# Attention decode step with gated Mish block: 4 MB loads in five buffers, wider projections and one merge of the row maxima

## Chip, cores and metric

The kernel runs on one core of a Trainium2 chip. The metric is the device time of one execution in microseconds. Before the change the median of three timed runs is 225.47 us (225.37 to 225.68). All data are float32.

## What is computed

Two batch rows, one new token each. `A` is attention over the last W = 4096 positions of a cache with 8 key/value heads, each shared by 4 of the 32 query heads; `B` is a two-layer block with a Mish activation; a scalar gate per batch row mixes them.

```
W = 4096; rep = 4; Dh = 128; D = 512; F = 1792
q = (x @ wq).reshape(B, 1, 32, 128).transpose(0, 2, 1, 3)
k = repeat(k_cache[:, :, Sk - W:, :], rep, axis=1)
v = repeat(v_cache[:, :, Sk - W:, :], rep, axis=1)
p = softmax(einsum("bhqd,bhkd->bhqk", q, k) * Dh ** -0.5)
a = einsum("bhqk,bhkd->bhqd", p, v).transpose(0, 2, 1, 3).reshape(B, 1, 4096) @ wo
h = x @ w1 + b1
b = (h * tanh(softplus(h))) @ w2
g = sigmoid((x * gate_w).sum(-1, keepdims=True))
out = g * a + (1 - g) * b
```

The host cuts and reorders the arrays before the launch, so that each load reads one contiguous piece of memory, with one contiguous row per partition.

## The kernel before, in words

**Loads.** Every large input goes through `load` (L49), which takes one of 20 buffers of 128 x 2048 floats (1 MB, a row of 8 KB per partition) and issues one DMA on SyncE (SP) at L51. For each of the 8 key/value heads there are four loads of keys (`k`, transposed on the host), four of values (`v`), one of the query weights (`wq`) and one of the output weights (`wo`). The hidden weights `w1` come in four loads of 896 KB, `w2` in nine loads cut at `CUTS` (L35), the last five of 256 KB with rows of 2 KB. SP issues in program order; a tile framework adds the waits for free buffers. With `sm`, a load of 13 KB that holds x, the gate weights and the bias, and the store of the result, there are 95 DMAs.

**Compute.** `x32` is x, padded to 32 columns, so that a matmul writes a group of 32 output partitions; four groups `j` make 128 partitions. `queries` (L113) projects x for one head: 16 matmuls of 128 columns, a copy, a transpose and two copies into `qz`. `softmax` (L130) makes the scores in 16 matmuls of 512 columns (L134), takes each row's maximum (L138), merges the maxima of the partitions that hold parts of the same row by a matmul and a masked minimum (L140, L143), and takes the exponential with its sum (L147); L149 to L154 make the reciprocal of the sum times the gate. `values` (L157) transposes the probabilities (L161), copies them (L162), does 16 matmuls of 512 columns with the values (L166), copies the result (L170) and gathers the diagonal blocks by four small matmuls (L177). `project` (L184) multiplies by `wo`: for each of the four query heads four matmuls of 128 columns into `acc`, through `accumulate` (L94). `hidden` (L188) does the first layer and Mish; `output` (L239) adds the second layer into the same `acc`.

**Order.** The loop at L245 issues, for head kv, its value loads, then the query weights and keys of the next head and that head's softmax, then `values` and `project`. The last head ends with `w2`, interleaved with two `wo` loads; the five 256 KB pieces of `w2` come last. Then four copies on VectorE bring `acc` into `res` (L270), and SP stores it (L271).

Of the kernel before, what the change touches and what calls it, by code (L numbers as in the profile page):

```python
# [8 lines left out]
F32 = mybir.dt.float32  # L9
# [17 lines left out]
Q = 32  # L27
F = 1792
DC = D // P
FC = F // P  # L30
FG = 4
SMALL = DC * B + DC + FC
SCALE = DH ** -0.5
BIG = 3.0e38
CUTS = (0, 2, 5, 7, 9, 10, 11, 12, 13, 14)  # L35
# [3 lines left out]
def decode_kernel(ctx: ExitStack, tc: tile.TileContext, small, wq, kt, v, wo, w1, w2, out):  # L39
# [3 lines left out]
    stream = ctx.enter_context(tc.tile_pool(name="stream", bufs=20))  # L43
# [10 lines left out]
    wq_t = load(wq[0], 2048, "wq0")  # L54
# [4 lines left out]
    b1 = sm[:, DC * B + DC :]  # L59

    ident = const.tile([P, P], F32, name="ident")
    make_identity(nc, ident)
    nident = const.tile([P, P], F32, name="nident")
    nc.vector.tensor_scalar_mul(nident, ident, -SCALE)
    fold = const.tile([P, Q], F32, name="fold")
    nc.vector.tensor_reduce(fold, ident.rearrange("p (j r) -> p r j", r=Q), axis=AX.X, op=ALU.add)
    key = const.tile([P, 2 * B, REP], F32, name="key")
    nc.vector.tensor_tensor(
        key,
        fold.rearrange("p (y n h) -> p y n h", n=NH, h=REP)[:, :, 0, :],  # L70
        fold.rearrange("p (y n h) -> p y n h", n=NH, h=REP)[:, :, 1, :], op=ALU.add)
    mask = const.tile([P, P], F32, name="mask")
    mv = mask.rearrange("p (j y n h) -> p j y n h", j=NJ, n=NH, h=REP)
    for j in range(NJ):
        for n in range(NH):
            nc.vector.tensor_scalar(mv[:, j, :, n, :], key, -BIG, BIG, op0=ALU.mult, op1=ALU.add)
# [11 lines left out]
    nc.gpsimd.memset(actT, 0.0)  # L88

    acc = ps_1.tile([P, P], F32, tag="acc", name="acc")  # L90
    n_acc = HQ + FC
    done = [0]

    def accumulate(lhsT, rhs):  # L94
        for j in range(NJ):
            nc.tensor.matmul(  # L96
                acc[Q * j : Q * j + Q, :], lhsT, rhs[:, j * P : (j + 1) * P],
                start=(done[0] == 0), stop=(done[0] == n_acc - 1),
            )
        done[0] += 1  # L100

    zp = ps_1.tile([P, B], F32, tag="q", name="zp")
    for c in range(DC):
        nc.tensor.matmul(zp, gw[:, c : c + 1].to_broadcast([P, P]), xT[:, c, :],
                         start=(c == 0), stop=(c == DC - 1))
    g = const.tile([P, B], F32, name="g")
    omg = const.tile([P, B], F32, name="omg")
    nc.scalar.activation(g, zp, AF.Exp, scale=-1.0)  # L108
    nc.vector.tensor_scalar_add(g, g, 1.0)
    nc.vector.reciprocal(g, g)  # L110
    nc.vector.tensor_scalar(omg, g, -1.0, 1.0, op0=ALU.mult, op1=ALU.add)

    def queries(kv, wq_t):  # L113
        qp = ps_1.tile([P, DH], F32, tag="q", name=f"qp{kv}")
        w = wq_t.rearrange("p (c n) -> p c n", c=DC)
        for c in range(DC):
            for h in range(REP):
                nc.tensor.matmul(qp[Q * h : Q * h + Q, :], x32[:, c, :],  # L118
                                 w[:, c, h * DH : (h + 1) * DH],
                                 start=(c == 0), stop=(c == DC - 1))  # L120
        qs = work.tile([P, DH], F32, tag="qs", name=f"qs{kv}")
        nc.vector.tensor_copy(qs, qp)
        qt = ps_1.tile([P, REP, Q], F32, tag="q", name=f"qt{kv}")
        nc.tensor.transpose(qt.rearrange("p h r -> p (h r)"), qs, ident)
        for n in range(NH):
            nc.vector.tensor_copy(
                qz[:, kv, :].rearrange("p (b n x) -> p b n x", n=NH, x=Q + REP)[:, :, n, :REP],
                qt.rearrange("p h r -> p r h")[:, :B, :])

    def softmax(kv, kts):  # L130
        sc = ps_s.tile([P, 512], F32, tag="sc", name=f"sc{kv}")
        for m in range(BN):
            for j in range(NJ):
                nc.tensor.matmul(sc[Q * j : Q * j + Q, :], qz[:, kv, m * Q : m * Q + Q],  # L134
                                 kts[m][:, j * 512 : (j + 1) * 512],
                                 start=(m == 0), stop=(m == BN - 1))
        mx = tiny.tile([P, 1], F32, tag="mx", name=f"mx{kv}")
        nc.vector.tensor_reduce(mx, sc, axis=AX.X, op=ALU.max)  # L138
        mb = ps_1.tile([P, P], F32, tag="mb", name=f"mb{kv}")
        nc.tensor.matmul(mb, mx.to_broadcast([P, P]), nident, start=True, stop=True)  # L140
        junk = work.tile([P, P], F32, tag="junk", name=f"junk{kv}")
        bias = tiny.tile([P, 1], F32, tag="bias", name=f"bias{kv}")
        nc.vector.tensor_tensor_reduce(out=junk, in0=mb, in1=mask, op0=ALU.add, op1=ALU.min,  # L143
                                       scale=1.0, scalar=BIG, accum_out=bias)
        p = work.tile([P, 512], F32, tag="p", name=f"p{kv}")
        l = tiny.tile([P, 1], F32, tag="l", name=f"l{kv}")
        nc.scalar.activation(p, sc, AF.Exp, bias=bias, scale=SCALE, accum_out=l)  # L147
        rl = tiny.tile([P, B, REP], F32, tag="rl", name=f"rl{kv}")
        nc.vector.tensor_scalar_mul(rl, key[:, :B, :], l)  # L149
        lp = ps_1.tile([P, B, REP], F32, tag="mb", name=f"lp{kv}")  # L150
        nc.tensor.matmul(lp, ones, rl, start=True, stop=True)  # L151
        r = tiny.tile([P, B, REP], F32, tag="r", name=f"r{kv}")
        nc.vector.reciprocal(r, lp)
        nc.vector.tensor_tensor(r, r, g[:, :, None].to_broadcast([P, B, REP]), op=ALU.mult)  # L154
        return p, r

    def values(kv, p, r, vts, between=None):  # L157
        pp = ps_1.tile([P, NT, P], F32, tag="pt", name=f"pp{kv}")
        pT = work.tile([P, NT, P], F32, tag="pT", name=f"pT{kv}")
        for t in range(NT):  # L160
            nc.tensor.transpose(pp[:, t, :], p[:, t * P : (t + 1) * P], ident)  # L161
        nc.vector.tensor_copy(pT, pp)  # L162
        o = ps_1.tile([P, BN * DH], F32, tag="o", name=f"o{kv}")
        for t in range(NT):
            for j in range(NJ):
                nc.tensor.matmul(o[Q * j : Q * j + Q, :], pT[:, t, Q * j : Q * j + Q],  # L166
                                 vts[t][:, j * 512 : (j + 1) * 512],
                                 start=(t == 0), stop=(t == NT - 1))
        os = work.tile([P, BN * DH], F32, tag="os", name=f"os{kv}")
        nc.scalar.copy(os, o)  # L170
        if between is not None:
            between()
        ol = ps_1.tile([P, B, REP], F32, tag="ol", name=f"ol{kv}")
        for b in range(B):
            for n in range(NH):
                m = b * NH + n
                nc.tensor.matmul(ol[:, b], os[:, m * DH : (m + 1) * DH],  # L177
                                 fold[:, m * REP : (m + 1) * REP],
                                 start=(n == 0), stop=(n == NH - 1))
        nc.vector.tensor_tensor(  # L180
            oT[:, kv * REP : (kv + 1) * REP, :B].rearrange("p h b -> p b h"), ol, r,
            op=ALU.mult)

    def project(kv, wo_t):  # L184
        for h in range(REP):
            accumulate(oT[:, kv * REP + h, :], wo_t[:, h * D : (h + 1) * D])

    def hidden(w1s):  # L188
        hp = ps_1.tile([P, FG * P], F32, tag="pt", name="hp")
        for c in range(DC):  # L190
            for j in range(NJ):
                n = min(FG, FC - j * FG) * P
                nc.tensor.matmul(hp[Q * j : Q * j + Q, :n], x32[:, c, :],  # L193
                                 w1s[c][:, j * FG * P : j * FG * P + n],
                                 start=(c == 0), stop=(c == DC - 1))
        hs = const.tile([P, FG * P], F32, name="hs")
# [3 lines left out]
        ht = ps_1.tile([P, FG, NJ, Q], F32, tag="q", name="ht")  # L200
# [29 lines left out]
    def head(kv, wq_t):  # L230
        kts = [load(kt[kv, m], 2048, f"k{kv}_{m}") for m in range(BN)]
        queries(kv, wq_t)
        return softmax(kv, kts)

    def load_w2(f0, n):
        src = w2[f0 * P * D : (f0 + n) * P * D].rearrange("(p x) -> p x", p=P)
        return f0, n, load(src, n * D, f"w2_{f0}")

    def output(loaded):  # L239
        f0, n, t = loaded  # L240
        for k in range(n):
            accumulate(actT[:, f0 + k, :], t[:, k * D : (k + 1) * D])

    st = head(0, wq_t)
    for kv in range(HKV):  # L245
        vts = [load(v[kv, t], 2048, f"v{kv}_{t}") for t in range(NT)]
        if kv == 1:
            hidden([load(w1[c * P : (c + 1) * P, :], F, f"w1_{c}") for c in range(DC)])
        nxt = head(kv + 1, load(wq[kv + 1], 2048, f"wq{kv + 1}")) if kv + 1 < HKV else None
        if kv < HKV - 2:  # L250
            wo_t = load(wo[kv], REP * D, f"wo{kv}")
        elif kv == HKV - 1:
# [7 lines left out]
        if kv == HKV - 1:  # L260
            project(kv - 1, wo_p)
        if kv != HKV - 2:
            project(kv, wo_t)
# [48 lines left out]
```

## Time and profile before

| what | value |
|---|---|
| median of the timed runs | 225.47 us |
| profiled execution: time shown by its profile (its span) | 223.8 us |
| instructions in the profile | 3067, of them 1316 matmuls and 1316 weight loads |
| PE busy / VectorE / ScalarE | 151.0 / 30.3 / 12.6 us |
| read from memory | 91.24 MB |
| mean granted TensorE clock | 0.794 |

The profiled execution has no timed value of its own; its span is 1.7 us below the median of the timed runs. In the page, the row GB/s gives what the DMA engines moved in 40 equal slices of the span; the row of a queue gives packets, megabytes and the share of the time of 16 DMA engines (where packets overlap a little, that share can pass 100%). A group's row gives busy time, mean duration in ns, and the idle time of the engine before it with what ended it. A row of the waits gives the total in us, how often, and the longest.

### The profile page before, as it was taken

To read this page: it belongs to the slowest core of one execution; us is meant where nothing else is said; L and a number is where in the kernel's file an instruction comes from. 1 tells how busy PE (TensorE), PEld (TensorE's weight loads), DVE (VectorE), ACT (ScalarE), POOL (GpSimd) and SP (SyncE) were. 2 spreads that over 40 slices of the span, in tenths; PEclk is the share of its full clock that TensorE was granted. 3 is DMA by queue.
4 is the path that set the end of the run, shared out by engine and by line. 5 is a ranking of instruction groups with operands and counts; after the bars stand their busy time and mean duration, and the time that the engine had idled before them with its cause. 6 is when DMAs were issued, how large, how long until landed. Compare 5 with 4: busy or idle time off the path is not lost.

```text
span 223.8 us, 3067 instructions
## 1 busy us (share of the span) xinstructions
PE 151.0 (67%) x1316; PEld 59.8 (27%) x1316; DVE 30.3 (14%) x128; ACT 12.6 (6%) x27; POOL 3.0 (1%) x9
## 2 busy tenths in 40 slices
PE   0794477503899687577975787568865786549662
PEld 0622051200043413014240523024322414031440
DVE  0403010200070211012010210021011201030002
ACT  2001010100001101001010101010100000010100
POOL 5000000000000000000000000000000000000000
PEclk9999967965699859855598559955899569955999
DMA  6999999999999999999999999999999999999980
GB/s 235 428 428 428 422 431 426 425 425 423 432 422 425 428 431 425 428 425 429 422 426 426 431 423 426 425 431 425 428 425 429 423 429 425 428 426 425 420 334 7
DMA packets 13552, 91.43 MB, mean 409 GB/s; under 512 B 1634, under 2 KB 1634, under 8 KB 3300
## 3 DMA queue, kind: packets, MB, share of 16 engines
q1 hardware_dynamic: 13540, 91.25, 97.1%
q8 instruction: 10, 0.16, 0.3%
q14 instruction: 2, 0.02, 0.0%
HBM read 91.24 MB, written 0.00 MB: 408 GB/s over the span
## 4 chain that ended last, share of the span: by engine, by line
DMA 96%; PE 1%; SPq 1%; DVE 1%; issue 0%; DVEq 0%
DMA k<-in_kt 49%; DMA v<-in_v 17%; DMA w<-in_w 12%; DMA wo<-in_wo 9%; DMA wq<-in_wq 9%; SPq L51 1%; PE sc L134 0%; DVE res L270 0%; DVE mx L138 0%; PE mb L140 0%; PE acc L96 0%; SPq L56 0%; DVEq L308 0%
## 5 line engine op out<-in xcount | busy, mean ns | idle before, releaser
L134 PE MATMUL sc<-k,qz 128*32 128x512 f32 x256 | 40.5, 717 | 18.7 <-DMA k<-in_kt 16.7
L166 PE MATMUL o<-v,pT 128*32 128x512 f32 x256 | 44.9, 836 | 8.4 <-DVE pT L162 5.5
L166 PEld LDWEIGHTS o<-v,pT 128*32 128x32 f32 x256 | 9.4, 145 | 38.2 <-issue 20.4
L134 PEld LDWEIGHTS sc<-k,qz 128*32 128x32 f32 x256 | 6.9, 120 | 43.1 <-DMA k<-in_kt 28.2
L96 PE MATMUL acc<-wo,oT 128*32 128x128 f32 x256 | 15.7, 355 | 2.2 <-DMA wo<-in_wo 2.2
L193 PE MATMUL hp<-w,x 128*32 128x512 f32 (+1 forms) x32 | 6.8, 853 | 10.1 <-DMA w<-in_w 10.1
L138 DVE TENSOR_REDUCE mx<-sc 128x1 f32<-128x512 f32 x8 | 5.5, 692 | 54.5 <-PE sc L134 54.5
L177 PE MATMUL ol<-fold,os 128*128 128x4 f32 x64 | 8.9, 262 | 4.6 <-ACT os L170 4.5
L177 PEld LDWEIGHTS ol<-fold,os 128*128 128x128 f32 x64 | 8.2, 201 | 11.2 <-ACT os L170 11.2
L96 PEld LDWEIGHTS acc<-wo,oT 128*32 128x32 f32 x256 | 9.8, 135 | 4.4 <-issue 2.7
L147 ACT ACTIVATE p<-sc,bias 128x512 f32<-128x512 f32 x8 | 5.5, 688 | 93.9 <-DVE bias L143 93.9
L118 PE MATMUL qp<-wq,x 128*32 128x128 f32 x256 | 10.4, 312 | 0.3 <-ACT g L108 0.3
L161 PE MATMUL pp<-ident,p 128*128 128x128 f32 x32 | 8.4, 398 | 2.5 <-ACT p L147 2.5
L180 DVE TENSOR_TENSOR oT<-ol,r 128x8 f32<-128x8 f32 x8 | 1.4, 172 | 61.7 <-PE ol L177 61.7
L140 PE MATMUL mb<-nident,mx 128*128 128x128 f32 x16 | 5.2, 417 | 6.5 <-DVE mx L138 6.5
L170 ACT COPY os<-o 128x512 f32<-128x512 f32 x8 | 4.7, 586 | 74.2 <-PE o L166 74.2
L118 PEld LDWEIGHTS qp<-wq,x 128*32 128x32 f32 x256 | 7.7, 124 | 0.9 <-ACT g L108 0.3
L140 PEld LDWEIGHTS mb<-nident,mx 128*128 128x128 f32 x16 | 3.2, 249 | 16.3 <-DVE mx L138 16.3
L162 DVE COPY pT<-pp 128x512 f32<-128x512 f32 x8 | 5.5, 692 | 10.5 <-PE pp L161 10.4
L96 PE MATMUL acc<-w,actT 128*32 128x128 f32 x112 | 4.9, 280 | 2.7 <-DMA w<-in_w 2.6
L161 PEld LDWEIGHTS pp<-ident,p 128*128 128x128 f32 x32 | 5.3, 205 | 4.9 <-ACT p L147 3.0
L151 PE MATMUL lp<-rl,ones 128*128 128x8 f32 x16 | 4.0, 322 | 3.7 <-DVE rl L149 3.7
(56 smaller groups left out, 41.6 us busy)
## 6 DMA issues: line engine op xcount, KB each, us to landing
k<-in_kt SPq DMA_DIRECT2D x32, 1024.0 KB, 19.6
v<-in_v SPq DMA_DIRECT2D x32, 1024.0 KB, 19.6
wq<-in_wq SPq DMA_DIRECT2D x8, 1024.0 KB, 19.6
wo<-in_wo SPq DMA_DIRECT2D x8, 1024.0 KB, 19.6
w<-in_w SPq DMA_DIRECT2D x4, 896.0 KB, 18.9
w<-in_w SPq DMA_DIRECT2D x3, 512.0 KB, 18.0
w<-in_w SPq DMA_DIRECT2D x5, 256.0 KB, 11.0
w<-in_w SPq DMA_DIRECT2D x1, 768.0 KB
```

Of the source, the lines that this page charges most:

```text
L96: nc.tensor.matmul(acc[Q * j : Q * j + Q, :], lhsT, rhs[:, j * P : (j + 1) * P], start=(done[0] == 0), stop=(done[0] == n_acc - 1),)
L118: nc.tensor.matmul(qp[Q * h : Q * h + Q, :], x32[:, c, :], w[:, c, h * DH : (h + 1) * DH], start=(c == 0), stop=(c == DC - 1))
L134: nc.tensor.matmul(sc[Q * j : Q * j + Q, :], qz[:, kv, m * Q : m * Q + Q], kts[m][:, j * 512 : (j + 1) * 512], start=(m == 0), stop=(m == ...
L138: nc.vector.tensor_reduce(mx, sc, axis=AX.X, op=ALU.max)
L140: nc.tensor.matmul(mb, mx.to_broadcast([P, P]), nident, start=True, stop=True)
L147: nc.scalar.activation(p, sc, AF.Exp, bias=bias, scale=SCALE, accum_out=l)
L161: nc.tensor.transpose(pp[:, t, :], p[:, t * P : (t + 1) * P], ident)
L162: nc.vector.tensor_copy(pT, pp)
L166: nc.tensor.matmul(o[Q * j : Q * j + Q, :], pT[:, t, Q * j : Q * j + Q], vts[t][:, j * 512 : (j + 1) * 512], start=(t == 0), stop=(t == NT ...
L170: nc.scalar.copy(os, o)
L177: nc.tensor.matmul(ol[:, b], os[:, m * DH : (m + 1) * DH], fold[:, m * REP : (m + 1) * REP], start=(n == 0), stop=(n == NH - 1))
L193: nc.tensor.matmul(hp[Q * j : Q * j + Q, :n], x32[:, c, :], w1s[c][:, j * FG * P : j * FG * P + n], start=(c == 0), stop=(c == DC - 1))
```

## The change

All tiles of the stream become 128 x 8192 floats (4 MB, a row of 32 KB per partition), in five buffers instead of 20 of a quarter the size. Keys and values are one load per head each, the query weights two loads of four heads each, `w1` one load; `w2` is cut at 10, 12 and 13, and its last three pieces go to buffers of their own. `wo` comes at the end of the stream, in loads of 4, 2, 1 and 1 heads. The host arrays follow these shapes. There are 29 DMAs instead of 95.

`queries` is done twice, for four heads at a time, with 512-column matmuls. `softmax` subtracts each partition's own maximum; the maxima of all heads are merged once at the end, in the new function `weights`, which also makes the factors that correct for it. `values` gathers the diagonal blocks on VectorE (`pick`) instead of PE. `outputs` applies the factors, and `project` does one 512-column matmul per query head into one of four partition groups, which `finish(fold, asum)` adds up at the end. The result's four copies are shared by VectorE and ScalarE. The program has 1,610 PE instructions instead of 2,670.

```diff
-CUTS = (0, 2, 5, 7, 9, 10, 11, 12, 13, 14)
+HALF = 4
+CHUNK = 8192
+CUTS = (0, 10, 12, 13, 14)
...
-    stream = ctx.enter_context(tc.tile_pool(name="stream", bufs=20))
+    stream = ctx.enter_context(tc.tile_pool(name="stream", bufs=5))
...
-        t = stream.tile([P, 2048], F32, tag="s", name=name)
+        t = stream.tile([P, CHUNK], F32, tag="s", name=name)
...
+    def queries(i, t):
+        w = t.rearrange("p (c k n) -> p c k n", c=DC, k=HALF)
+        qp = ps_1.tile([P, REP * DH], F32, tag="o", name=f"qp{i}")
         for c in range(DC):
...
+            for k in range(HALF):
+                nc.tensor.matmul(qp[Q * k : Q * k + Q, :], x32[:, c, :], w[:, c, k, :],
                                  start=(c == 0), stop=(c == DC - 1))
...
+        nc.vector.tensor_reduce(mx[:, kv : kv + 1], sc, axis=AX.X, op=ALU.max)
         bias = tiny.tile([P, 1], F32, tag="bias", name=f"bias{kv}")
...
+        nc.vector.tensor_scalar_mul(bias, mx[:, kv : kv + 1], -SCALE)
         p = work.tile([P, 512], F32, tag="p", name=f"p{kv}")
...
+        nc.scalar.activation(p, sc, AF.Exp, bias=bias, scale=SCALE, accum_out=ls[:, kv : kv + 1])
...
+        d = od[:, kv, :]
+        nc.vector.tensor_scalar_mul(d, o[:, 0, :], pick[:, 0:1])
+        for m in range(1, BN):
+            nc.vector.scalar_tensor_tensor(d, o[:, m, :], pick[:, m : m + 1], d,
+                                           op0=ALU.mult, op1=ALU.add)
...
+    def weights():
+        mt = ps_1.tile([HKV, NJ, Q], F32, tag="q", name="mt")
+        nc.tensor.transpose(mt.rearrange("k j r -> k (j r)"), mx, ident)
...
+        for j in range(NJ):
+            nc.vector.tensor_tensor(mj[:, j], m4[:, j, :, 0, :], m4[:, j, :, 1, :], op=ALU.max)
+        top = const.tile([HKV, Q // NH // REP, REP], F32, name="top")
+        nc.vector.tensor_reduce(top, mj.rearrange("k j y h -> k y h j"), axis=AX.X, op=ALU.max)
+        for j in range(NJ):
+            for n in range(NH):
+                nc.vector.tensor_tensor(m4[:, j, :, n, :], m4[:, j, :, n, :], top, op=ALU.subtract)
+        nc.scalar.activation(ms, ms, AF.Exp, scale=SCALE)
...
+    queries(0, wq_a)
+    queries(1, wq_b)
+    hidden(w1_t)
+
+    for kv in range(HKV - 1):
+        pT = softmax(kv, load(kt[kv], CHUNK, f"k{kv}"))
+        values(kv, pT, load(v[kv], CHUNK, f"v{kv}"))
...
+    w2_0 = load_w2(0)
+    wos = [(k0, k1, load_wo(k0, k1)) for k0, k1 in ((0, 4), (4, 6), (6, 7), (7, 8))]
+    tail = [load_w2(i) for i in range(1, len(CUTS) - 1)]
...
+    def project(j, lhsT, rhs, n):
+        nc.tensor.matmul(acc[Q * j : Q * j + Q, :], lhsT, rhs,
+                         start=(n_col[j] == 0), stop=(n_col[j] == n - 1))
...
+    nc.scalar.copy(asum[:, : D // 2], acc[:, : D // 2])
+    nc.vector.tensor_copy(asum[:, D // 2 :], acc[:, D // 2 :])
...
+    output(1)
+    finish(fold, asum)
+    output(2)
+    output(3)
...
     for j in range(NJ):
-        nc.vector.tensor_copy(res[:, j * P : (j + 1) * P], acc[Q * j : Q * j + B, :])
+        copy = nc.scalar.copy if j % 2 else nc.vector.tensor_copy
+        copy(res[:, j * P : (j + 1) * P], fin[Q * j : Q * j + B, :])
```

On SP, the loads at the start of the program; the number after the partitions is the floats of a row. Before, the query weights of one head, the small load `sm`, and the keys and values of the first head:

```order
L51 DMA wq_73<-in_wq 128x2048
L56 DMA sm<-in_small 128x26
L51 DMA k_0_120<-in_kt 128x2048
L51 DMA k_1_122<-in_kt 128x2048
L51 DMA k_2_124<-in_kt 128x2048
L51 DMA k_3_126<-in_kt 128x2048
L51 DMA v_0_185<-in_v 128x2048
```

After, on SP at the same place:

```order
L53 DMA wqa<-in_wq 128x8192
L58 DMA sm<-in_small 128x26
L53 DMA wqb<-in_wq 128x8192
L53 DMA w_79<-in_w 128x7168
L53 DMA k_231<-in_kt 128x8192
L53 DMA v_262<-in_v 128x8192
L53 DMA k_285<-in_kt 128x8192
```

All query weights and `w1` (`w_79`) now stand ahead of the first keys, and the sixth large load (`k_285`) is the first that reuses a buffer.

On SP, the loads at the end of the program. Before, `w` with an underscore is a piece of `w2`, named by its first block:

```order
L51 DMA wo_1111<-in_wo 128x2048
L51 DMA w_2_1113<-in_w 128x1536
L51 DMA w_5_1115<-in_w 128x1024
L51 DMA w_7_1117<-in_w 128x1024
L51 DMA w_9_1119<-in_w 128x512
L51 DMA w_10_1121<-in_w 128x512
L51 DMA w_11_1123<-in_w 128x512
L51 DMA w_12_1125<-in_w 128x512
L51 DMA w_13_1127<-in_w 128x512
L271 DMA out<-res 2x512
```

After, on SP from the last head's keys on:

```order
L53 DMA k_609<-in_kt 128x8192
L53 DMA v_611<-in_v 128x8192
L53 DMA w_0_613<-in_w 128x5120
L53 DMA wo_615<-in_wo 128x8192
L53 DMA wo_617<-in_wo 128x4096
L53 DMA wo_619<-in_wo 128x2048
L53 DMA wo_621<-in_wo 128x2048
L261 DMA w_10_623<-in_w 128x1024
L261 DMA w_12_625<-in_w 128x512
L261 DMA w_13_627<-in_w 128x512
L322 DMA out<-res 2x512
```

All of `wo` has moved behind the last values, and the last 1 MB is three pieces of `w2` instead of five with 1.25 MB. Counting five buffers back, `wo_619` takes the buffer of the last keys and `wo_621` that of the last values.

On PE, the end of the program after the change, from the last head's scores on (`mt`, `ft`, `lp` belong to `weights`, `ol` to `outputs`):

```order
L130 MATMUL sc_631<-k_609,qz 32x512 x16
L141 MATMUL pp_653<-ident,p_651 128x128 x4
L185 MATMUL lp<-kl,ones 128x64
L195 MATMUL ol<-kf,od 128x8 x7
L149 MATMUL o_706<-v_611,pT_654 32x512 x16
L277 MATMUL acc<-w_0_613,actT 32x512 x10
L277 MATMUL acc<-wo_615,oT 32x512 x16
L277 MATMUL acc<-wo_621,oT 32x512 x4
L287 MATMUL fin<-w_10_623,actT 32x128 x8
L287 MATMUL fin<-asum,fold 32x128 x4
L287 MATMUL fin<-w_12_625,actT 32x128 x4
L287 MATMUL fin<-w_13_627,actT 32x128 x4
```

Where `wo` of a head was used right after that head's values before, all of it is now used here; between the last of it and the last two pieces of `w2` stand the copies into `asum` and the four matmuls that add it up.

More of the change, by code (lines that the diff above doesn't have):

```diff
@@ L88, in decode_kernel @@
     nc.gpsimd.memset(actT, 0.0)
[L90 to L115, printed above, removed]
+    mx = const.tile([P, HKV], F32, name="mx")
+    ls = const.tile([P, HKV], F32, name="ls")
@@ L120, in queries @@
                                  start=(c == 0), stop=(c == DC - 1))
-        qs = work.tile([P, DH], F32, tag="qs", name=f"qs{kv}")
+        qs = work.tile([P, REP * DH], F32, tag="p", name=f"qs{i}")
         nc.vector.tensor_copy(qs, qp)
[L123 to L128, printed above, removed]
@@ L130, in softmax @@
-    def softmax(kv, kts):
+        qt = ps_1.tile([P, REP, HALF, Q], F32, tag="pt", name=f"qt{i}")
+        for h in range(REP):
+            nc.tensor.transpose(qt[:, h].rearrange("p k r -> p (k r)"),
+                                qs[:, h * DH : (h + 1) * DH], ident)
+        for k in range(HALF):
+            for n in range(NH):
+                nc.vector.tensor_copy(
+                    qz[:, i * HALF + k, :].rearrange("p (b n x) -> p b n x", n=NH, x=Q + REP)[:, :, n, :REP],
+                    qt[:, :, k, :B].rearrange("p h b -> p b h"))
@@ L131, in softmax @@
+    def softmax(kv, t):
         sc = ps_s.tile([P, 512], F32, tag="sc", name=f"sc{kv}")
@@ L145, in softmax @@
         p = work.tile([P, 512], F32, tag="p", name=f"p{kv}")
[L146 to L157, printed above, removed]
+        nc.scalar.activation(p, sc, AF.Exp, bias=bias, scale=SCALE, accum_out=ls[:, kv : kv + 1])
         pp = ps_1.tile([P, NT, P], F32, tag="pt", name=f"pp{kv}")
         pT = work.tile([P, NT, P], F32, tag="pT", name=f"pT{kv}")
-        for t in range(NT):
-            nc.tensor.transpose(pp[:, t, :], p[:, t * P : (t + 1) * P], ident)
+        for c in range(NT):
+            nc.tensor.transpose(pp[:, c, :], p[:, c * P : (c + 1) * P], ident)
@@ L162, in values @@
         nc.vector.tensor_copy(pT, pp)
-        o = ps_1.tile([P, BN * DH], F32, tag="o", name=f"o{kv}")
-        for t in range(NT):
+        return pT
+    def values(kv, pT, t):
+        o = ps_1.tile([P, BN, DH], F32, tag="o", name=f"o{kv}")
+        for c in range(NT):
             for j in range(NJ):
-                nc.tensor.matmul(o[Q * j : Q * j + Q, :], pT[:, t, Q * j : Q * j + Q],
-                                 vts[t][:, j * 512 : (j + 1) * 512],
-                                 start=(t == 0), stop=(t == NT - 1))
@@ L169, in values @@
[L169 to L173, printed above, removed]
-        for b in range(B):
[L175 to L189, printed above, removed]
+                nc.tensor.matmul(o[Q * j : Q * j + Q], pT[:, c, Q * j : Q * j + Q],
+                                 t[:, (c * NJ + j) * 512 : (c * NJ + j + 1) * 512],
+                                 start=(c == 0), stop=(c == NT - 1))
@@ new lines, in outputs, with hidden @@
+    def outputs(ol, kf, r, k0, k1):
+        for kv in range(k0, k1):
+            nc.tensor.matmul(ol[:, kv].rearrange("p b h -> p (b h)"), od[:, kv, :], kf[:, kv, :],
+                             start=True, stop=True)
+        for b in range(B):
+            nc.vector.tensor_tensor(
+                oT.rearrange("p (k h) x -> p k h x", h=REP)[:, k0:k1, :, b],
+                ol[:, k0:k1, b, :], r[:, k0:k1, b, :], op=ALU.mult)
+    def hidden(t):
+        w = t[:, : DC * F].rearrange("p (c f) -> p c f", c=DC)
+        hp = ps_1.tile([P, FG * P], F32, tag="o", name="hp")
@@ L228, in hidden @@
                                 op=ALU.mult)
[L230 to L252, printed above, removed]
-            tail = []
-            for f0, f1 in zip(CUTS, CUTS[1:]):
-                tail.append(load_w2(f0, f1 - f0))
-                if f0 == 0:
-                    wo_p = load(wo[kv - 1], REP * D, f"wo{kv - 1}")
-                    wo_t = load(wo[kv], REP * D, f"wo{kv}")
-        values(kv, *st, vts, between=(lambda: output(tail[0])) if kv == HKV - 1 else None)
[L260 to L263, printed above, removed]
-        st = nxt
@@ L265, in decode_kernel, with load_w2 @@
-    for x in tail[1:]:
-        output(x)
+    queries(0, wq_a)
[4 more added lines that the diff above has]
+        values(kv, pT, load(v[kv], CHUNK, f"v{kv}"))
+    last_k = load(kt[HKV - 1], CHUNK, "k7")
+    last_v = load(v[HKV - 1], CHUNK, "v7")
+    def load_w2(i):
+        f0, f1 = CUTS[i], CUTS[i + 1]
+        src = w2[f0 * P * D : f1 * P * D].rearrange("(p x) -> p x", p=P)
+        if i == 0:
+            return load(src, (f1 - f0) * D, f"w2_{f0}")
+        t = const.tile([P, (f1 - f0) * D], F32, name=f"w2_{f0}")
+        nc.sync.dma_start(t, src)
+        return t
@@ new lines, in decode_kernel, with finish @@
+    n_of = [HKV + len(range(j, CUTS[1], NJ)) for j in range(NJ)]
+    n_fin = FC - CUTS[1] + 1
+    done = [0]
+    def finish(lhsT, rhs):
+        for j in range(NJ):
+            nc.tensor.matmul(fin[Q * j : Q * j + Q, :], lhsT, rhs[:, j * P : (j + 1) * P],
+                             start=(done[0] == 0), stop=(done[0] == n_fin - 1))
+        done[0] += 1
+    pT = softmax(HKV - 1, last_k)
+    kf, r = weights()
+    ol = ps_1.tile([P, HKV, B, REP], F32, tag="q", name="ol")
+    outputs(ol, kf, r, 0, HKV - 1)
@@ new lines, in decode_kernel @@
+    values(HKV - 1, pT, last_v)
+    for f in range(CUTS[1]):
+        project(f % NJ, actT[:, f, :], w2_0[:, f * D : (f + 1) * D], n_of[f % NJ])
+    outputs(ol, kf, r, HKV - 1, HKV)
+    for k0, k1, t in wos:
+        for kv in range(k0, k1):
+            for h in range(REP):
+                x = ((kv - k0) * REP + h) * D
+                project(h, oT[:, kv * REP + h, :], t[:, x : x + D], n_of[h])
+    asum = const.tile([P, D], F32, name="asum")
+    nc.scalar.copy(asum[:, : D // 2], acc[:, : D // 2])
@@ L268, in decode_kernel, with output @@
+    nc.vector.tensor_copy(asum[:, D // 2 :], acc[:, D // 2 :])
+    def output(i):
+        for f in range(CUTS[i], CUTS[i + 1]):
+            x = (f - CUTS[i]) * D
+            finish(actT[:, f, :], tail[i - 1][:, x : x + D])
+    output(1)
+    finish(fold, asum)
+    output(2)
+    output(3)
     res = const.tile([B, D], F32, name="res")
     for j in range(NJ):
-        nc.vector.tensor_copy(res[:, j * P : (j + 1) * P], acc[Q * j : Q * j + B, :])
+        copy = nc.scalar.copy if j % 2 else nc.vector.tensor_copy
+        copy(res[:, j * P : (j + 1) * P], fin[Q * j : Q * j + B, :])
```

103 lines of the change are left out of this document (68 added, 35 removed).

## Prediction

> **What bounds the kernel now.** I read the page first: its rows of DMA, the queues and the chain that ended last.
>
> ```profile
> PEclk9999967965699859855598559955899569955999
> DMA  6999999999999999999999999999999999999980
> GB/s 235 428 428 428 422 431 426 425 425 423 432 422 425 428 431 425 428 425 429 422 426 426 431 423 426 425 431 425 428 425 429 423 429 425 428 426 425 420 334 7
> ...
> q8 instruction: 10, 0.16, 0.3%
> ...
> HBM read 91.24 MB, written 0.00 MB: 408 GB/s over the span
> ...
> DMA 96%; PE 1%; SPq 1%; DVE 1%; issue 0%; DVEq 0%
> ...
> k<-in_kt SPq DMA_DIRECT2D x32, 1024.0 KB, 19.6
> ```
>
> The DMA engines are full from the second slice to the 38th, the chain is DMA for 96% of the span, and TensorE (PE) is 67% busy. So the time is start + bytes over rate + what follows the last byte. The rows of the groups count only where they reach into the start or the end.
>
> What one load costs is read from two windows of the DMA view, one in which every row is 8 KB (27 to 46 us) and one of the 256 KB loads with rows of 2 KB (214.3 to 216 us).
>
> ```profile
> DMA packets 1116, 8.13 MB, mean 428 GB/s; under 512 B 124, under 2 KB 124, under 8 KB 124
> ...
> DMA packets 355, 0.69 MB, mean 405 GB/s; under 512 B 40, under 2 KB 40, under 8 KB 355
> ```
>
> Of 1116 packets 124 are small: eight rows and one small packet for each load on each of 16 engines, in both windows alike. 1 MB at 428 GB/s is 2.450 us, and 256 KB at 405 GB/s is 0.647 us. Two loads that differ only in the length of their rows give a fixed and a growing part: (2.450 - 0.647) / 0.75 = 2.404 us for each MB, and 0.046 us for each load, whatever its size.
>
> Then the end of the stream, 215.9 to 219.9 us, in slices of 0.1 us, and the microsecond from 217.85 us:
>
> ```profile
> GB/s 471 389 328 307 389 266 266 246 307 205 225 225 246 184 164 225 143 164 123 307 21 41 21 20 20 41 20 20 20 41 41 21 20 20 41 0 0 0 0 0
> ...
> q1 hardware_dynamic: 308, 0.54, 35.6%
> ...
> q1 hardware_dynamic: 21, 0.03, 9.1%
> q8 instruction: 1, 0.02, 5.9%
> ```
>
> The 16 engines don't finish together. Full is 405 GB/s, so one engine is 25. By 217.9 us all but one or two are done, and these go on to 219.4 us. Spread evenly, the 0.54 MB of q1 would have ended at 215.9 + 0.54 / 405 GB/s = 217.2 us; the last engine is 2.2 us behind that. In the second window lies one of the ten instruction packets of the page (16 KB each): it holds one engine for 5.9% of 16 us, 0.94 us. Ten such packets over 16 engines explain an end of this shape: engines with none, with one, and one or two that got a second.
>
> Last, the end of the timeline, and the clock there:
>
> ```profile
> 219.94 0.43 PE L96 MATMUL acc<-w,actT 128*32 128x128 f32 x8 [0.38 <-DMA w<-in_w]
> 220.44 1.18 DVE L270 COPY res<-acc 2x128 f32<-2x128 f32 x4 [10.96 <-PE acc L96]
> ...
> 210.00:219.00 9.00, 5.45 (x144) 3.32 (x138) 0.00 (x0) 0.00 (x0) 0.00 (x0) 1.00 0.83 330
> ```
>
> **The change, part by part.** *Fewer loads.* There are 28 loads instead of 94 for the same bytes, and each still gives an engine eight rows and one small packet. 66 x 0.046 us = 3.0 us less stream; the new rate in the middle would be 4 MB / (4 x 2.404 + 0.046) = 434 GB/s. No row of this trace shows a load packet over 8 KB, so the cost is bounded: if a row of 32 KB went as four packets of 8 KB, only the small packet goes, one of nine, 66 x 0.005 = 0.3 us. That longer packets are slower isn't excluded either (rival 2). I take 3.0 us: it is the line through the two measured row lengths, and the nearer of them, 8 KB, shows no falling off.
>
> The Trainium skill, page "DMA: Bandwidth & Descriptors", section "Anatomy of one DMA", gives a DMA some 2.0 us fixed beside bytes over 436 GB/s; 66 loads fewer would be 132 us by that. Here a load takes 19.6 us from issue to landing while one lands every 2.45 us, so the fixed latency is hidden behind the loads in flight and I count none of it.
>
> *Fewer instruction packets.* The ten packets are 0.16 MB for the 2,670 PE instructions, 60 bytes each; 1,610 make 0.10 MB, six packets. Six over 16 engines seldom meet twice on one. If none does, the last engine ends where all but one or two end now, 217.9 instead of 219.4 us: 1.5 us less. Bounds: 0, if two meet again, and 2.2 us plus a sixteenth of four packets (0.2 us), if the engines end together. I take 1.5 us.
>
> *After the last byte.* The last load feeds four matmuls (8 instructions) before and after. The four copies of 1.18 us are shared by VectorE and ScalarE, two each: 0.6 us less. ScalarE's copy of such a small tile isn't in the trace; its nearest rows are these:
>
> ```profile
> L170 ACT COPY os<-o 128x512 f32<-128x512 f32 x8 | 4.7, 586 | 74.2 <-PE o L166 74.2
> L108 ACT ACTIVATE g<-zp 128x2 f32<-128x2 f32 x1 | 0.2, 173 | 5.8 <-PE zp L104 5.8
> ```
>
> Two at 173 to 586 ns are 0.35 to 1.17 us against VectorE's 0.59 us, so the gain is 0 to 0.6 us. A tile a quarter as long as the first row's lies nearer 280 ns, so VectorE's pair ends last: 0.6 us.
>
> *The merged tail.* After the last `wo` load PE does four wide matmuls, the accumulator is copied in halves, and four matmuls add it up, ahead of the last two pieces of `w2` in PE's order. Three loads of 512, 256 and 256 KB land behind that `wo` load: 1 x 2.404 + 3 x 0.046 = 2.54 us of cover. The work:
>
> ```profile
> L193 PE MATMUL hp<-w,x 128*32 128x512 f32 x24 | 6.8, 946 | 10.1 <-DMA w<-in_w 10.1
> L198 DVE COPY hs<-hp 128x256 f32<-128x256 f32 x1 | 0.4, 425 | 17.3 <-PE hp L193 17.3
> ```
>
> Four wide matmuls run side by side in about 0.95 us, the half copy takes 0.43, the four narrow ones 0.43, with three hand-overs of some 0.1 us: 2.1 us, inside 2.54. The clock was 1.00 in this stretch; at half of it PE's share doubles, 3.5 us, and the end would be 1.0 us later. I take 0, bounds 0 and +1.0.
>
> *Five buffers.* A load waits for the matmuls that read the load five before it, so a buffer may be held for about four loads, 4 x 9.66 = 39 us, less some 1 us from issue to data. Held how long:
>
> ```profile
> L166 PE MATMUL o<-v,pT 128*32 128x512 f32 x256 | 44.9, 836 | 8.4 <-DVE pT L162 5.5
> L134 PE MATMUL sc<-k,qz 128*32 128x512 f32 x256 | 40.5, 717 | 18.7 <-DMA k<-in_kt 16.7
> L138 DVE TENSOR_REDUCE mx<-sc 128x1 f32<-128x512 f32 x8 | 5.5, 692 | 54.5 <-PE sc L134 54.5
> L147 ACT ACTIVATE p<-sc,bias 128x512 f32<-128x512 f32 x8 | 5.5, 688 | 93.9 <-DVE bias L143 93.9
> L161 PE MATMUL pp<-ident,p 128*128 128x128 f32 x32 | 8.4, 398 | 2.5 <-ACT p L147 2.5
> L162 DVE COPY pT<-pp 128x512 f32<-128x512 f32 x8 | 5.5, 692 | 10.5 <-PE pp L161 10.4
> L154 DVE TENSOR_TENSOR r<-r,g 128x8 f32<-128x8 f32 x8 | 1.3, 164 | 0.2
> ```
>
> A head is 40.5/8 + 0.69 + 0.69 + 8.4/8 + 0.69 + 44.9/8 = 13.8 us of the 19.3 us that its keys and values take to land. No stall in the loop. The tightest place is the load `wo_621`, which waits for the last values to be read. The last head's scores, its softmax and the new function `weights` stand before that: 8.2 us, some 24 small VectorE steps at 0.16 us (3.9) with a few small matmuls, hand-overs and an exponential (about 3), then 5.6 us of values, 20.7 us after the last keys. Between those keys and `wo_621` 4 + 2.5 + 4 + 2 + 1 = 13.5 MB land, 32.5 us; 1 us for the issue leaves 11 us of cover. If it failed, SP would stand at that load, and the three `w2` pieces behind it on its queue too. The projections' narrower or wider matmuls, the VectorE gathers and the smaller load `sm` behind the first 4 MB are all under the stream: nothing.
>
> Sum: 3.0 + 1.5 + 0.6 = 5.1 us. The profiled span becomes 223.8 - 5.1 = 218.7 us; the median of the timed runs is 1.7 us above the span, so 220.4 us.
>
> **The rivals.** *1. The rows are cut.* The hardware moves 32 KB as packets of 8 KB. The rate stays 428 GB/s, the first term is 0.3: 225.5 - 0.3 - 1.5 - 0.6 = 223.1 us. For it: no longer load packet is seen. Against: a row is one packet at 2 KB and at 8 KB, as eight rows to each small packet show in the two windows, and instruction packets are 16 KB. Chance 0.15.
>
> *2. Longer rows are slower (the other side).* The engines' reading points lie 32 KB times the rows between them apart, four times as far as before; if they meet in memory, or a packet of 32 KB moves worse than four of 8 KB, the rate falls. It decides from the point where the stream loses the 2.1 us of the two other terms: 91.24 MB at 428 GB/s is 213.2 us, at 215.3 us it is 424 GB/s, 1% less. At 420 GB/s, the lowest full slice of the page (the 38th), it is 217.2 us: +4.0 - 2.1, so 227.4 us. For it: a 16 KB packet took 0.94 us, 17 GB/s on an engine that otherwise moves 27, though it came from another queue and shared the engine. Against: the rate rises from rows of 2 KB to rows of 8 KB. Chance 0.13.
>
> The Trainium skill speaks here, page "DMA: Bandwidth & Descriptors", section "Latency and other measured facts": copies whose rows lie 512 KB apart in memory ran at 207 instead of 214 GB/s, and worse farther apart. Its 3% would be an estimate of 7 us here and 230 us in all. This change stays at 32 KB, where the page has no figure, and no run yet shows one.
>
> *3. The buffers come back late.* PE at half clock, which the page's row shows as 5 in single slices, doubles the 11.7 us of matmuls of the tail: 20.7 + 11.7 = 32.4 us, beyond the 31.5 us, so the stream stands still for 0.9 us, and the merge adds up to 1.0 us: 222.3 us. Against: the clock is 9 in the last slices. Chance 0.04.
>
> **The numbers.** The forecast has 0.68. Its own range goes down to 219.3 us (0.7 + 0.2 us for an end that all engines reach together, 0.2 us for the rounding of the two rates) and up to 221.9 (no gain from the instruction packets). Rival 1 ends at 223.1, and a few tenths for its tail give 223.4; rival 3 lies inside. Outside stay rival 2 and the far ends of the others, some 0.2 together. About 0.2% (0.45 us) is what a measurement of this kernel can tell from no change; of rival 2, 0.03 falls within that near its break-even point, and 0.10 is slower. Faster is the rest, 0.68 + 0.15 + 0.04 = 0.87.
>
> **What would show it.** Right: GB/s near 434 in the middle slices, q8 with six packets, a last slice pair without a tail of one engine at 25 GB/s of over 0.5 us, two copies each on VectorE and ScalarE, and SP waiting for PE only with loads still in flight. Wrong: 428 in the middle (rival 1), less (rival 2), zeros in the DMA row or waits of SP for `o` before `wo_621` (rival 3), or `fin` waiting for `asum` after the last `w2` landed.

## The result and the profile after

The changed kernel takes 221.51 us (median of 4 runs, 221.27 to 222.26) against 225.42 us before, measured beside it; the ratio is 0.9833, 95% interval 0.9818 to 0.9847. It is faster by 3.9 us where 5.1 were forecast. The profiled execution's span went from 223.8 to 219.7 us.

The page of the changed kernel, the rows that answer to those of before:

```profile
span 219.7 us, 1885 instructions
...
PEclk9999988887969976676969799585888879679999
DMA  7999999999999999999999999999999999999990
GB/s 280 406 462 397 454 431 427 441 419 465 400 465 394 462 400 459 412 447 430 430 444 418 453 412 453 406 465 403 453 406 453 424 436 407 440 462 403 409 381 22
...
q8 instruction: 6, 0.10, 0.2%
...
k<-in_kt SPq DMA_DIRECT2D x8, 4096.0 KB, 43.0
```

DMA is as full as before and bounds the kernel still. The slices of GB/s swing more, because a packet of 32 KB is counted whole in the slice where it starts; a long window gives the rate. The DMA view from 80 to 200 us, of before and then of after:

```profile
DMA packets 7024, 51.19 MB, mean 427 GB/s; under 512 B 781, under 2 KB 781, under 8 KB 781
```

```profile
DMA packets 1831, 52.02 MB, mean 433 GB/s; under 512 B 194, under 2 KB 194, under 8 KB 194
```

The rate rose from 427 to 433 GB/s; 434 was forecast. There are still about eight other packets to each small one (1637 to 194, with those cut by the window's ends), so a row of 32 KB is one packet. Now the end of the stream in slices of 0.1 us, from 211.8 us in the changed kernel:

```profile
GB/s 573 389 348 410 410 246 451 451 369 369 512 389 348 451 471 287 328 225 184 184 143 205 184 164 143 164 164 123 164 123 123 82 21 20 41 0 0 0 0 0
```

By the packet records the last of these packets ends at 215.4 us, before at 219.5: 4.1 us, which is the whole difference of the spans. What follows it takes 4.3 us, as before. The stretch in which one or two engines run alone (20 to 41 GB/s) has shrunk from 15 slices to three. What follows the last byte shows in the timeline:

```profile
215.43 0.74 PE L287 MATMUL fin<-w,actT 128*32 128x128 f32 x14
216.24 0.28 DVE L321 COPY res<-fin 2x128 f32<-2x128 f32 x1 [1.01 <-PE fin L287]
216.55 0.26 ACT L321 COPY res<-fin 2x128 f32<-2x128 f32 x1 [1.78 <-DVE res L321]
216.84 0.28 DVE L321 COPY res<-fin 2x128 f32<-2x128 f32 x1 [0.32 <-ACT res L321]
217.16 0.26 ACT L321 COPY res<-fin 2x128 f32<-2x128 f32 x1 [0.35 <-DVE res L321]
```

The four copies are shared by two engines and still stand in a row: each waits for the one before it on the other engine (`<-DVE res`, `<-ACT res`). They take 1.18 us, as before.

### The profile page after: what moved, and what is told of

Same layout as the page of the kernel before. It is cut to its first block, busy times and chain, and to the rows that moved or that the text cites. A ratio compares the mean times of both kernels' runs of the same rounds, so it can differ in the third digit from the quotient of the medians.

```text
span 219.7 us, 1885 instructions
## 1 busy us (share of the span) xinstructions
PE 123.8 (56%) x798; PEld 37.0 (17%) x798; DVE 36.5 (17%) x132; ACT 9.1 (4%) x23; POOL 3.0 (1%) x9
## 4 chain that ended last, share of the span: by engine, by line
DMA 80%; PE 15%; DVE 2%; ACT 1%; SPq 1%; issue 1%; DVEq 0%
DMA k<-in_kt 40%; DMA w<-in_w 21%; DMA v<-in_v 19%; PE sc L130 5%; PE o L149 4%; PE hp L208 2%; PE ol L195 1%; PE fin L287 1%; SPq L53 1%; ACT p L137 0%; DVE mx L133 0%; DVE pT L142 0%; PE pp L141 0%; DVE res L321 0%; DVE r L188 0%
## 5 line engine op out<-in xcount | busy, mean ns | idle before, releaser
L149 PE MATMUL o<-v,pT 128*32 128x512 f32 x256 | 40.5, 790 | 12.1 <-DMA v<-in_v 11.3
L130 PEld LDWEIGHTS sc<-k,qz 128*32 128x32 f32 x256 | 9.9, 147 | 68.8 <-DMA k<-in_kt 42.8
L112 PE MATMUL qp<-wqa,x 128*32 128x512 f32 x32 | 6.6, 763 | 13.5 <-DVE x L79 13.5
L141 PE MATMUL pp<-ident,p 128*128 128x128 f32 x32 | 5.5, 297 | 14.4 <-ACT p L137 14.4
L277 PE MATMUL acc<-wo,oT 128*32 128x512 f32 x64 | 7.7, 598 | 4.2 <-DMA wo<-in_wo 4.2
L155 DVE SCALAR_TENSOR_TENSOR od<-o,pick,od 128x128 f32<-128x128 f32 x24 | 8.4, 351 | 0.8
L195 PE MATMUL ol<-kf,od 128*128 128x8 f32 x16 | 3.5, 350 | 2.3 <-DVE od L155 1.6
L112 PE MATMUL qp<-wqb,x 128*32 128x512 f32 x32 | 3.6, 594 | 0.9 <-DMA wqb<-in_wq 0.9
L195 PEld LDWEIGHTS ol<-kf,od 128*128 128x128 f32 x16 | 3.4, 312 | 3.4 <-DVE od L155 2.6
L277 PEld LDWEIGHTS acc<-wo,oT 128*32 128x32 f32 x64 | 1.7, 109 | 10.2 <-DMA wo<-in_wo 5.5
```

The lines of the kernel that those rows point to most:

```text
L112: nc.tensor.matmul(qp[Q * k : Q * k + Q, :], x32[:, c, :], w[:, c, k, :], start=(c == 0), stop=(c == DC - 1))
L141: nc.tensor.transpose(pp[:, c, :], p[:, c * P : (c + 1) * P], ident)
L149: nc.tensor.matmul(o[Q * j : Q * j + Q], pT[:, c, Q * j : Q * j + Q], t[:, (c * NJ + j) * 512 : (c * NJ + j + 1) * 512], start=(c == 0), s ...
L155: nc.vector.scalar_tensor_tensor(d, o[:, m, :], pick[:, m : m + 1], d, op0=ALU.mult, op1=ALU.add)
L195: nc.tensor.matmul(ol[:, kv].rearrange("p b h -> p (b h)"), od[:, kv, :], kf[:, kv, :], start=True, stop=True)
L277: nc.tensor.matmul(acc[Q * j : Q * j + Q, :], lhsT, rhs, start=(n_col[j] == 0), stop=(n_col[j] == n - 1))
```

## The experiments

The theory: the stream is shorter because each load has a fixed price and because fewer instruction packets hold up single DMA engines; the copies gained nothing because of their waits. The main rival: the load size does nothing, and the time came from PE's lighter work.

**Every load in quarters.** The changed kernel with loads of 1 MB into the same buffers:

```diff
-        nc.sync.dma_start(t[:, :cols], src)
+        for x in range(0, cols, 2048):
+            n = min(2048, cols - x)
+            nc.sync.dma_start(t[:, x : x + n], src[:, x : x + n])
```

> The changed kernel with every load cut into loads of at most 128 x 2048 floats into the same five buffers; PE, VectorE and ScalarE do the same work. Theory (a load has a fixed price of about 0.046 us, whatever its rows' length): 66 loads more, so the middle runs at 428 GB/s again and the time is 221.5 + 3.0 = 224.5 us. Rival (the gain came from the fewer PE instructions and their packets): the time stays at 221.5 us.

Measured: 224.62 us (median of 10, 223.72 to 225.45), 3.1 us above the changed kernel. The DMA view of this run from 80 to 200 us:

```profile
DMA packets 7094, 51.21 MB, mean 427 GB/s; under 512 B 782, under 2 KB 782, under 8 KB 910
```

The old rate is back, with PE's work as light as in the changed kernel, and the rival falls. The cut adds 63 loads, not the 66 of the expectation: there are 91 against 28, since `w2` comes in six pieces here and came in nine before. Not all of the 3.1 us is the loads'. In the profiled execution, 224.73 us against 221.49, the last load packet ends at 217.6 us instead of 215.4: 2.2 us. The other 1.0 us lies behind it, where PE's last matmuls ran at a granted clock of 0.50 instead of 1.00 (more on this under "The merged tail" below). Three microseconds around the end of the stream, of the changed kernel and then of this run:

```profile
213.00:216.00 3.00, 2.62 (x48) 1.29 (x48) 0.42 (x1) 0.37 (x1) 0.00 (x0) 1.00 0.37 145
```

```profile
215.00:218.00 3.00, 2.46 (x24) 1.08 (x26) 0.07 (x1) 0.37 (x1) 0.00 (x0) 0.50 0.56 220
```

Such a row gives a stretch and its length, the busy time of PE, its weight loads, VectorE, ScalarE and GpSimd, then the granted clock, the share of the DMA engines and GB/s. The three fastest of the ten executions, 223.72 to 223.79 us, are also 2.2 to 2.3 us above the changed kernel.

**One load, short rows.** The host stores each 4 MB as four blocks; one load reads 512 rows of 8 KB:

```diff
+        if cols == CHUNK:
+            s4 = src.rearrange("p c -> (p c)").rearrange("(a p c) -> p a c", p=P, c=2048)
+            nc.sync.dma_start(t.rearrange("p (a c) -> p a c", c=2048), s4)
```

> The changed kernel with its loads of 4 MB kept, but stored on the host in four blocks, so that one load reads 512 rows of 8 KB instead of 128 of 32 KB. The theory splits here. If the fixed price belongs to each row's packet (0.046 us over nine packets, 0.005 each), 19 loads with 24 more packets on each engine cost 19 x 24 x 0.005 = 2.3 us: 223.8 us. If it belongs to the load, nothing changes: 221.5 us.

Measured: 223.37 us (223.35 to 224.44), 1.9 us above the changed kernel. Its DMA view, same window:

```profile
DMA packets 6274, 51.38 MB, mean 428 GB/s; under 512 B 197, under 2 KB 197, under 8 KB 197
```

Now 31 packets of data stand to one small packet, and the rate is 428. On each engine 19 loads have 24 packets more; 1.9 us over these is 0.004 us for a packet. The packet records are sharper. Where no instruction packet falls between, 4 MB follow 4 MB every 9.681 us in the changed kernel, every 9.794 us here, and every 9.812 us in the run with quarters (4 x 2.453). So 24 more packets on each engine cost 0.113 us, 0.005 us each, and three more loads another 0.018 us: about six sevenths of the price belong to the rows' packets, and the rest is the load's own.

**More PE instructions.** Tiny matmuls per head, into a PSUM tile of their own (n = 33, then 16):

```diff
+        for i in range(n):
+            nc.tensor.matmul(spare[:Q, :], pT[:, 0, :Q], ident[:, :8],
+                             start=(i == 0), stop=(i == n - 1))
...
+    junk = const.tile([Q, 8], F32, name="junk")
...
+    nc.vector.tensor_copy(junk, spare[:Q, :])
```

> The changed kernel with 33 tiny matmuls added per head (32 x 8, into a tile that only an unused copy reads), so that the program has some 2,670 PE instructions again. Theory (each 16 KB of PE instructions takes one DMA engine away for a while, and the stream ends with its last engine): ten instruction packets instead of six, two engines get a second one and end about 1.4 us later: 222.9 us. Rival (PE's instruction count is free as long as PE waits for data): 221.5 us and an unchanged end of the stream.

> As the run with 33 tiny matmuls per head, but with 16: some 2,120 PE instructions and eight instruction packets. If the packets go round the engines in turn, no engine gets a second one yet and the time stays at 221.5 us; if each packet costs the same share of the time, it is half of the larger run's loss, 222.2 us; if they fall at random, two on one engine are likely and the time is up to 222.9 us.

Measured: 223.81 us with 33 (223.64 to 224.26) and 222.57 with 16 (222.35 to 223.47). The ends of their streams, 4 us in slices of 0.1, first the run with 33 from 213.9 us, then the run with 16 from 213.2 us:

```profile
GB/s 430 328 389 369 205 184 430 103 164 246 287 184 246 184 225 246 143 205 225 143 143 21 61 41 41 61 61 41 41 61 41 61 41 61 21 0 0 0 0 0
```

```profile
GB/s 266 389 369 389 451 328 471 430 307 369 348 246 287 143 246 205 266 184 246 225 266 184 184 225 205 205 143 82 21 0 0 0 0 0 0 0 0 0 0 0
```

With ten instruction packets a tail of 1.4 us returns, one to three engines alone; with eight there is none. That is the shape of packets that go round the engines, eight before one gets its second. But both runs lost about 1 us more than this tail explains.

**The same once more, and its parts.** In the packet records of both runs a packet of 32 KB took 1.216 us instead of 1.213, and a load of 4 MB 9.720 instead of 9.681 us (medians), from 36 to 40 us on, while the first keys land.

> The run with 33 tiny matmuls per head once more, unchanged: its packets of 32 KB took 0.3% longer than those of the changed kernel from the first keys on, which the instruction count doesn't explain. If that comes from the program, the time is 223.8 us again and the rate in the middle is the same; if it came from where that execution's data lay, the packets are as fast as the changed kernel's and the time is 221.5 + 1.4 = 222.9 us.

> As the run with 33 tiny matmuls per head, but its copy goes into a tile that the kernel has anyway, so no tile in SBUF is added and the buffers of the loads lie where the changed kernel has them. If the packets were 0.3% longer because the added tile of 32 bytes moved the buffers, the middle is back at the changed kernel's rate and only the second instruction packets cost: 222.9 us. If the matmuls or their number are the cause: 223.9 us again.

> As the run with 33 tiny matmuls per head and the tile of 32 bytes, but with one tiny matmul per head, so some 1,640 PE instructions and six instruction packets. If the added tile made the packets longer: 221.5 + 0.9 = 222.4 us. If the number of PE instructions did: 221.5 us.

Of the last two runs the first copies into `od`, which exists anyway, instead of `junk`; the second keeps `junk` and has n = 1. Beside these two the changed kernel ran again, on the same chip; the repeat with 33 ran on another:

> The changed kernel once more, on the chip of the three runs beside it: 221.5 us, packets of 32 KB one after the other every 1.210 us, six instruction packets on six engines.

| run | PE instructions | tile of 32 bytes | us (range) |
|---|---|---|---|
| changed kernel again | 1,610 | no | 221.38 (221.32 to 222.37) |
| n = 33, no tile | about 2,670 | no | 222.75 (222.57 to 222.90) |
| n = 1, tile | about 1,640 | yes | 222.41 (222.33 to 222.47) |
| n = 33, tile, again | about 2,670 | yes | 223.97 (223.84 to 224.78) |

The four fit two prices that add: 1.4 us for the ten instruction packets, as forecast, and 1.0 us for the added tile of 32 bytes, whatever PE does. The run without the tile, its page and its end of the stream (4 us from 213.2):

```profile
q8 instruction: 10, 0.16, 0.3%
```

```profile
GB/s 451 389 266 266 287 164 246 225 184 225 246 225 205 225 205 184 225 102 82 61 82 20 41 41 82 41 41 41 82 41 41 41 61 20 20 0 0 0 0 0
```

Ten packets and the tail of one to four engines, from 215.0 to 216.7 us. The packet records of this run can be followed from packet to packet on each engine. The first eight instruction packets meet eight engines, the ninth meets the engine of the first and the tenth that of the second. Each puts the loads of its engine back by 1.42 us. In the changed kernel six meet six engines.

**The copies.** Two PSUM tiles and two result tiles, one for each engine, and two stores:

```diff
-    fin = ps_1.tile([P, P], F32, tag="fin", name="fin")
+    fins = [ps_1.tile([P, P], F32, tag=f"fin{i}", name=f"fin{i}") for i in range(2)]
...
+    rs = [const.tile([B, D // 2], F32, name=f"res{i}") for i in range(2)]
     for j in range(NJ):
+        copy = nc.scalar.copy if j // 2 else nc.vector.tensor_copy
+        copy(rs[j // 2][:, j % 2 * P : (j % 2 + 1) * P], fins[j // 2][Q * j : Q * j + B, :])
```

> The changed kernel with the final accumulator in two PSUM tiles of their own banks, the result in two tiles, VectorE copying one half and ScalarE the other, and two stores, one issued by SP and one by ScalarE. Theory (the four copies stand in a row because the two engines wait for each other on the shared tiles): the copies take 0.6 us instead of 1.18, so 221.5 - 0.6 = 220.9 us. Rival (the end is set by the store and what lies behind it): 221.5 us, or more with the second store.

Measured: 221.25 us (220.71 to 221.78), ratio to before 0.982 (0.9797 to 0.9844). Its timeline:

```profile
216.88 0.57 DVE L321 COPY res<-fin 2x128 f32<-2x128 f32 x2 [0.97 <-PE fin L287]
217.06 0.53 ACT L321 COPY res<-fin 2x128 f32<-2x128 f32 x2 [1.60 <-PE fin L287]
217.48 0.32 SPq L323 DMA_DIRECT2D out<-res  x1
217.62 0.53 ACTq L324 DMA_DIRECT2D out<-res  x1
```

Side by side the copies take 0.71 us, so the shared tiles were the cause of the row. The gain in time stays inside the scatter of the runs: inconclusive. Two executions took 220.71 and 220.86 us, two 221.65 and 221.78; the profiled one is the 221.65, and its clock was 0.50 from 213 to 216 us, as in the run with quarters. ScalarE's store, too, takes 0.53 us to issue against SP's 0.32.

One copy of the whole accumulator, four stores:

```diff
+    res = const.tile([P, P], F32, name="res")
+    nc.vector.tensor_copy(res, fin)
     for j in range(NJ):
+        q = nc.scalar if j % 2 else nc.sync
+        q.dma_start(o2[:, j * P : (j + 1) * P], res[Q * j : Q * j + B, :])
```

> The changed kernel with one VectorE copy of the whole 128 x 128 accumulator in place of the four, and four small stores, two issued by SP and two by ScalarE. Theory (a copy of 2 x 128 costs 0.28 us and one of 128 x 128 0.29 us, by rows of before): the copies take 0.3 us instead of 1.18, the second store of each queue adds 0.33: 221.5 - 0.55 = 220.95 us. Rival: four stores cost more at the end than the copies did, 221.5 us or more.

> The kernel with one copy and four stores once more, beside the changed kernel on the same chip. Theory (the copies are on the path): 0.6 us below the changed kernel, 220.9 us. Rival (its gain was the scatter between calls): the same time as the changed kernel.

Measured: 220.91 us (220.73 to 221.88), and 220.89 (220.85 to 221.72) beside the changed kernel's 221.38 on the same chip; ratios to before 0.9814 (0.9791 to 0.9837) and 0.9813 (0.9796 to 0.9830). The timeline of the second:

```profile
216.17 0.29 DVE L319 COPY res<-fin 128x128 f32<-128x128 f32 x1 [1.01 <-PE fin L287]
216.49 0.63 SPq L323 DMA_DIRECT2D out<-res  x2
216.49 0.83 ACTq L323 DMA_DIRECT2D out<-res  x2
```

One copy is 0.29 us in place of 1.18, and the second store of each queue gives back 0.3 to 0.5. The gain of about 0.5 us came twice; the intervals of this kernel and of the changed one still overlap. It is the fastest version measured.

**Two buffers instead of five** (`bufs=2` in the stream pool).

> The changed kernel with two buffers of 4 MB instead of five. Theory (a buffer must come back within the landing of one other load, 9.7 us, less 1 us for the issue): in the loop keys are held about 6 us and values 4 to 5 us, no stall; at the end the first wo load waits for the last values to be read, 19.8 us after the last keys landed, where the stream could have started it at 15.7: a stall of about 5 us, and a few tenths later on, so 227 us. Rival (4 MB loads need many buffers, every load then stalls by its latency of 1 us or more): 19 loads x 1 us or more, 240 us.

Measured: 241.07 us (240.38 to 242.56), near the rival's number, but only in part by its mechanism. The chain of this run, at the scores of the last two heads and at the end of PE's work; and the DMA view from 100 to 140 us:

```profile
164.68 6.27 PE sc L130 x32
...
185.50 6.10 PE sc L130 x32
...
208.08 2.72 PE acc L277 x20
210.81 13.62 DMA wo<-in_wo
...
226.46 4.73 DMA wo<-in_wo
```

```profile
DMA packets 570, 16.56 MB, mean 414 GB/s; under 512 B 64, under 2 KB 64, under 8 KB 64
...
q1 hardware_dynamic: 569, 16.55, 99.2%
```

The last scores start 7.5 us later than in the changed kernel (185.5 against 178.0). Of this 1.0 us was there at the first scores (43.6 against 42.6), and the rest is 0.9 us a head, with a rate of 414 GB/s. What follows the start of the last scores takes 53.3 us instead of 41.7. The wait for the last values, worked out at 5 us, is the first of four: `wo` of two heads waits for the first piece of `w2` to be used, the next `wo` for the first one, and the last `wo` for that of two heads. The working held for one load at a time and left out that a late load makes the next one's buffer late. Where the loop's 0.9 us a head come from, with DMA 99% busy by its packets, isn't settled. The packet records show where they lie: most packets take 1.213 us as ever, and some take up to 3.1 us, mostly among the first two that an engine gets of a new load. That is the rival's kind of loss, about half a microsecond a load.

## Why the prediction held, and where it missed

*What bounds the kernel:* right. DMA was full before and after; PE's busy time fell from 151.0 to 123.8 us; in the run with ten instruction packets and no tile it is back at 146.2 us, and what follows the stream still takes 4.3 us.

*Fewer loads, 3.0 us:* right in kind, somewhat too large. The rate came to 433 GB/s instead of 434. Cutting the loads again, 63 more of them, moves the end of the stream by 2.2 us. From before to the run with ten instruction packets and no tile, where the loads changed and the number of packets did not, the end moves from 219.5 to 216.7 us, 2.7 us by the records, and the medians by 225.3 - 222.75 = 2.6 us. The split by rows that the prediction could only bound (0.3 to 3.0 us) is measured: most of the price is the packet's.

*Fewer instruction packets, 1.5 us:* right. The mechanism is shown by the run that brings the packets back, 1.4 us, and by its packet records. From before to the run with quartered loads, where the packets changed and the number of loads hardly did (94 to 91), the end of the stream moves from 219.5 to 217.6 us, 1.9 us; the medians, 225.34 - 224.62 = 0.7 us, also hold the slower clock behind the stream. The new order of the loads lies in this comparison as well as in the one before, and no run separates its share.

*The copies, 0.6 us:* this is the step that failed; the forecast time came near because the two larger terms held. The prediction held that "the four copies of 1.18 us are shared by VectorE and ScalarE, two each: 0.6 us less". It priced ScalarE's copy rightly (0.26 us), and did not ask whether the two engines may work at once. They write one tile and read one PSUM bank, and each copy waits for the other engine's: 1.18 us, gain 0. Two tiles and two banks put them side by side.

The 3.9 us measured is then this. In the profiled executions the end of the stream moved by 4.1 us where 3.0 + 1.5 = 4.5 were forecast; the two pairs of runs split it into 2.7 + 1.4 or 2.2 + 1.9 us, loads and instruction packets. What follows the stream moved by 0 where 0.6 was forecast. So of the missing 1.2 us, 0.6 is the copies and 0.4 the stream, where the loads fell short by either split; the last 0.2 is the difference between the spans, 4.1 us, and the medians, 3.9 us, and lies within the scatter of the runs.

*The merged tail, 0:* right at full clock only. In the profiled execution of the changed kernel the accumulator's half copies also stand in a row, 0.37 + 0.42 us, but under the cover of the last `w2` loads: PE ends 0.8 us after the last packet, before 0.9. In that of its repeat, 222.37 us, the stream ends even earlier, at 215.1 us, but PE ends 2.0 us after it. The same stretch in the two, then the last matmuls of the repeat (0.74 us for the same 14 above):

```profile
214.00:217.00 3.00, 2.07 (x44) 1.10 (x40) 0.86 (x3) 0.63 (x2) 0.00 (x0) 1.00 0.13 51
214.00:217.00 3.00, 3.00 (x44) 2.12 (x40) 0.42 (x1) 0.37 (x1) 0.00 (x0) 0.51 0.12 47
215.85 1.23 PE L287 MATMUL fin<-w,actT 128*32 128x128 f32 x14
```

At a granted clock of 0.51 the merge sticks out behind the loads, and the execution took about 1.0 us more than the other three of that run (221.32 to 221.42); the prediction's bound was +1.0. One execution of the first run of the changed kernel, 222.26 us, lies as high; it has no profile, so that its cause is the same is likely and not shown.

*Five buffers, no stall:* right. The chain of the changed kernel has the landing of the last keys, the last values' matmuls and the issue that waited for them:

```profile
133.33 44.65 DMA k<-in_kt
178.02 5.38 PE sc L130 x32
...
192.81 4.95 PE o L149 x32
197.78 0.33 SPq L53
```

The tightest load was issued 19.8 us after the last keys had landed (177.98 to 197.78 us); 20.7 was forecast, of 31.5 that it had. The waits of SP for PE in the changed kernel's view are long and cost nothing:

```profile
SPq L53 <- PE o L149: 46.6, 8, 10.1
SPq L53 <- PE sc L130: 43.6, 8, 6.2
```

*The rivals:* rows cut into packets of 8 KB, no, by the count of packets; longer rows slower, no, 433 GB/s, so the Trainium skill's figures on rows at large pitch (page "DMA: Bandwidth & Descriptors", section "Latency and other measured facts") have no counterpart at 32 KB; buffers late, not with five, though the other half of that rival, a merge at half clock, does occur.

## What to carry to other kernels

Where DMA bounds a kernel, count the packets and the loads as well as the bytes, and look at how the stream ends: the last engine sets the time, and PE instructions cost time there though PE waits. Two engines that share a copy gain nothing while they share its tiles; read the waits before halving a duration. Work that just hides under the last loads at full clock may not hide at half of it, and one profile need not show both. Working out one buffer's hold time gives a safe yes with room to spare, but no price once it fails.

## What was not expected of the hardware

A tile of 32 bytes that nothing else uses cost 1.0 us (222.41 against 221.38 us), in the three programs that had it and not in the two otherwise alike without it. With it the load packets take longer, at 8, 16 and 32 KB alike by 3 to 4 ns in the median (309 to 313, 611 to 614, 1213 to 1216 ns). The cause is open. That the tile moves the buffers of the loads, and so their alignment, is a guess, and their place alone doesn't explain it. The longer packets begin only 36 to 40 us into the execution, while the first keys land, so that the same first buffer was filled at 1.213 us a packet by `wqa` and at 1.216 by the second head's keys. And the instruction packets, which don't go into these buffers, took 1.00 to 1.11 us with the tile and 0.88 to 0.97 without. The Trainium skill, page "DMA: Bandwidth & Descriptors", section "How a descriptor splits into AXI transactions", counts more beats for a descriptor that doesn't start at a multiple of 256 bytes, and says so of reading; no run here shows the addresses.
